# The first head of attention opened with transposes in place of shift transfers, and the end of attention in another order

## The chip, the cores and the metric

One core of a Trainium2 chip runs the whole program. The metric is the device time of one execution in microseconds; the kernel before took a median of 728.87 us in three runs (727.69 to 729.34).

## The reference

Three stages follow each other: attention that only looks at keys of the same hash bucket, a gated layer, and a layer of experts of which each token uses one. The change touches the first and the point where it meets the second.

```python
# q, k, v: [2, 8, 768, 64]; proj: [64, 6]
q_bits = (einsum('bhsd,dk->bhsk', q, proj) > 0)       # and k_bits alike
q_bucket = sum(q_bits * 2 ** arange(6), axis=-1)      # and k_bucket alike
mask = q_bucket[:, :, :, None] == k_bucket[:, :, None, :]
scores = where(mask, scale * q @ k.T, -1e9)
attn = softmax(scores)
x = (attn @ v) as [1536, 512]
x = ((x @ w_a) * (x @ w_b)) @ w_out                   # w_a, w_b: [512, 1536], w_out: [1536, 512]
out = experts(x)                                      # 8 experts, one per token, with a gate
```

## The kernel before

**Units.** Attention works on 8 pairs of heads (`pairs`; pair i has two heads j), each head in 3 units of 256 queries: 48 units, `NU`. In unit u two tiles of 128 queries (t = 0, 1) go through `scores` (L205: Q x K, with the sum over 64 numbers, for the two halves of the keys on the two row halves of TensorE; L208: a product of the sign bits, which lifts keys of the same bucket by a large number), `rowmax` on VectorE (L213), `expo` on ACT (L219), `normal` on GpSimd (L231), `turn` on VectorE (L238, a transpose in blocks of 32) and, in two groups of 12 blocks for each head, `pv` on TensorE (L250). The score banks are two tiles of `ps_s`; scores of unit u + 1 wait for the exponentials of unit u.

**Operands.** `load` fetches a pair's K and Q rows into `raw`; `turned` turns them with TensorE (L114) into K and Q, with the first head's 64 numbers on partitions 0 to 63 and the second's on 64 to 127. A score tile needs one half of the keys on the other 64 partitions: `swap` makes the shifted copies QS and KS with DMAs on SP (L104, L106). `signs` multiplies by the random directions (L181, L161 or L163) and takes signs on ACT (L154): sk for keys, from which KF is made by two factors (L145), and QF and QG for queries. For pair 0 all of this stands ahead of the loop over the units: K and Q are turned and evicted whole, four swaps are issued, the queries' signs are taken in four passes. For later pairs it is spread over the units.

**What sets the order.** Each engine runs its instructions in the order in which the program issues them; there is no scheduler. The loop over u in `attention` issues rows and exponentials, scores, preparations, transposes and pv, and calls `hook(u, place)` at five places. `tile_kernel` hangs other work there:

- `plan` and `places` hold the steps that split the first weights of the gated layer from 64-bit words into two 32-bit parts (`split64`): fetch (L431, SP), rest (L436) and top (L439) on VectorE, low (L445, ACT), add (L450, GpSimd), size (L455, ACT), guard (L461, VectorE), parts (L466 ACT, L467 GpSimd). The last two jobs (`outs`) are the halves of w_out; their scratch tile `late` lies in the buffer of `raw`, so it is free once the last pair is turned (unit 34), and the second half's fetch waits for the first half's parts.
- `fill` says after which units gated products are issued on TensorE (L536): a number 2 is one group of 12 matmuls over 384 columns. Up to unit 46 they use a bank of pv; from NU on a score bank. Their evictions are held back until the next `hook(u, 2)`.

The last units are: pv of head 14, first group, at u = 47 and second group at u = 48; two groups of pv of head 15 behind the loop, between `hook(NU + 2, 0)`, `hook(NU + 3, 0)` and `hook(NU + 4, 0)`. `epilogue` (L270) empties the pv banks of a head with four copies on ACT before the next head's pv may write them.

Of the kernel before, what the change touches and what calls it, by code (L numbers as in the profile page):

```python
# [8 lines left out]
F32 = mybir.dt.float32  # L9
F32R = mybir.dt.float32r  # L10
BF16 = mybir.dt.bfloat16
I32 = mybir.dt.int32
U32 = mybir.dt.uint32
AF = mybir.ActivationFunctionType
ALU = mybir.AluOpType
# [10 lines left out]
class Kernel:  # L26
# [37 lines left out]
    def attention(self, xh, xl, pools, hook):  # L64
        nc = self.nc
        sb, ps_s, ps_pv = pools
        NB = self.proj.shape[1]
        S, D = self.S, self.D
        NC = S // 128
# [3 lines left out]
        H2 = S // 2  # L73
# [6 lines left out]
        raw, Q, QS, K, KS, QF, QG, KF, VR = {}, {}, {}, {}, {}, {}, {}, {}, {}  # L80

        def load(i, qs=(nc.sync, nc.sync)):
            b, hp = pairs[i]
            t = raw[i] = sb.tile([128, 2, NC, 2, D], F32, tag="raw", name="raw", bufs=1)
            for j in range(2):
                for n, src in ((1, self.k), (0, self.q)):
                    qs[n].dma_start(out=t[:, n, :, j, :], in_=src[b, 2 * hp + j].rearrange("(p c) d -> p c d", c=NC))

        def load_v(h):
            (b, hp), j = pairs[h // 2], h % 2  # L90
# [10 lines left out]
        def swap(i, n, a):  # L101
            x, y = slice(64 * a, 64 * a + 64), slice(64 - 64 * a, 128 - 64 * a)
            if n == 0:
                nc.sync.dma_start(out=QS[i][x], in_=Q[i][y])  # L104
            else:
                nc.sync.dma_start(out=KS[i][x], in_=K[i][y, a * H2:(a + 1) * H2])  # L106
# [4 lines left out]
        def turned(i, n):  # L111
            p = pvb[n]
            for c in range(NC):
                nc.tensor.transpose(  # L114
                    p[:, c // 3, c % 3 * 128:c % 3 * 128 + 128], raw[i][:, n, c].rearrange("p h d -> p (h d)"), self.ident
                )
            if n == 0:
                Q[i] = sb.tile([128, S], F32, tag="q", name="q", bufs=2)
                QS[i] = sb.tile([128, S], F32, tag="qs", name="qs", bufs=2)
            else:  # L120
                K[i] = sb.tile([128, S], F32, tag="k", name="k", bufs=2)
                KS[i] = sb.tile([128, H2], F32, tag="ks", name="ks", bufs=2)
            dst = halves((Q, K)[n][i])

            def out(eng, swaps=True):
                scale = float(D) ** -0.5 if n == 0 else 1.0
                if eng is nc.scalar:
                    nc.scalar.mul(dst, p[:, :, :H2], scale)
                else:
                    eng.tensor_scalar(dst, p[:, :, :H2], scale, None, ALU.mult)  # L130
                if swaps:
                    for a in (1, 0):
                        swap(i, n, a)

            return out

        later = []

        def masks(eng=nc.scalar):
            for kf, sk in later:  # L140
                for j in range(2):
                    if eng is nc.scalar:
                        eng.mul(kf[:, j], sk, self.fac[:, j:j + 1])
                    else:
                        eng.tensor_scalar(kf[:, j], sk, self.fac[:, j:j + 1], None, ALU.mult)  # L145
            later.clear()

        def signs(i, n):
            p = pvb[n]
            lz = self.lz.rearrange("p a b c -> p (a b c)")  # L150
            half = [slice(64 * x, 64 * x + 64) for x in range(2)]

            def sign(dst, src):
                nc.scalar.activation(dst, src, AF.Sign, bias=self.bias[:src.shape[0]], scale=2.0 ** 100)  # L154

            if n == 0:
                QF[i] = sb.tile([128, H2], BF16, tag="qf", name="qf", bufs=2)
                QG[i] = sb.tile([128, H2], BF16, tag="qg", name="qg", bufs=2)
                for x, r in enumerate(half):
                    if i == 0:  # L160
                        nc.tensor.matmul(p[:, x, :H2], lz, Q[i][:, x * H2:(x + 1) * H2], start=True, stop=True)  # L161
                    else:
                        nc.tensor.matmul(  # L163
                            p[r, 0, :H2], lz[:, r], Q[i][:, x * H2:(x + 1) * H2], start=True, stop=True, tile_position=(0, 64 * x)
                        )

                def out(*_):
                    if i == 0:
                        for x in range(2):
                            sign(QF[i][half[x]], p[half[x], x, :H2])  # L170
                            sign(QG[i][half[1 - x]], p[half[1 - x], x, :H2])
                        return
                    sign(QF[i], p[:, 0, :H2])
                    for x in range(2):
                        nc.sync.dma_start(out=QG[i][half[1 - x]], in_=QF[i][half[x]])

                return out
            KF[i] = sb.tile([128, 2, H2], BF16, tag="kf", name="kf", bufs=2)
            sk = sb.tile([128, H2], BF16, tag="sk", name="sk", bufs=1)
            for x, r in enumerate(half):  # L180
                nc.tensor.matmul(  # L181
                    p[r, 0, :H2], lz[:, r], K[i][:, x * H2:(x + 1) * H2], start=True, stop=True, tile_position=(0, 64 * x)
                )

            def out(*_):
                sign(sk, p[:, 0, :H2])
                later.append((KF[i], sk))

            return out
# [94 lines left out]
        NU = len(units)  # L284
# [6 lines left out]
        for j in range(2):  # L291
            d = slice(64 * j, 64 * j + 64)
            for x in range(2):
                nc.vector.tensor_copy(self.lz[d, x, j, :NB], self.pr[d])
        turns = turned(0, 1), turned(0, 0)
        turns[0](nc.scalar, False)
        turns[1](nc.vector, False)
        for a in (1, 0):
            for n in (1, 0):
                swap(0, n, a)  # L300
        load(1)
        hook(-1, 0)
        load_v(0)
        preps = signs(0, 1), signs(0, 0)
        for prep in preps:
            prep()
        masks(nc.vector)
        scores(0, 0)
        scores(0, 1)
        preps = []  # L310
        finish = (
            (1, finish_add, (cols[0],)), (2, finish_add, (cols[1],)), (2, finish_high, (cols[0],)),
            (3, finish_low, (cols[0],)), (3, finish_high, (cols[1],)), (4, finish_low, (cols[1],)),
# [717 lines left out]
def tile_kernel(ctx, tc, q, k, v, proj, w_a, w_b, w_out, emb, tau, w1, w2, out, dbg=None):  # L1031
# [5 lines left out]
    with tc.manual_schedule():  # L1037
# [15 lines left out]
        with tc.tile_pool(name="conv", bufs=1, side="left") as X.conv, \  # L1053
                tc.tile_pool(name="att", bufs=2, side="right") as sb, \
                tc.tile_pool(name="ps_s", bufs=2, space=PSUM) as ps_s, \
                tc.tile_pool(name="ps_pv", bufs=1, space=PSUM) as ps_pv:

            def spare():
                return X.mid.tile([128, 4 * 384], F32R, tag="g", name="spare")

            def late():
                return sb.tile([128, 2 * S], F32, tag="raw", name="late", bufs=1)

            jobs = [X.load_first(w, f, spare) for f in range(2) for w in range(2)]
            outs = [X.load_first(2, f, late) for f in range(2)]


            plan = {(-1, 0): [jobs[0][0], jobs[1][0]], (36, 1): [outs[0][0]], (45, 1): [outs[1][0]]}
            places = (
                (3, 4, 5, 6, 6, 7, 9), (8, 8, 9, 10, 12, 13, 15), (16, 17, 18, 21, 21, 22, 27), (20, 23, 24, 28, 30, 31, 33),  # L1070
                (38, 38, 39, 40, 41, 41, 45), (NU, NU, NU, NU + 1, NU + 1, NU + 1, NU + 2),
            )
            for (_, steps), us in zip(jobs + outs, places):
                for m, u in enumerate(us):
                    plan.setdefault((u, 3 if m in (3, 4, 6) else 4), []).append(steps[m])
            plan[13, 0], plan[16, 0] = [jobs[2][0]], [jobs[3][0]]
            first = [(t, f, w, h) for t in range(2) for f in range(2) for w in range(2) for h in range(2)]


            fill = {40: 2, 43: 2, 46: 2, NU: 2, NU + 2: 2, NU + 3: 2, NU + 4: 4}  # L1080

            held = []

            def hook(u, at):
                if at == 2:
                    while held:
                        held.pop(0)()
                for job in plan.pop((u, at), []):
                    job()
                if at == 0:  # L1090
                    for n in range(fill.get(u, 0)):
                        t, f, w, half = first.pop(0)
                        if half == 0:
                            X.part = K.banks[(2, 0)[n // 2]] if u < NU else K.bank()
                        X.gated_products(0, t, f, w, half, X.part, held if u < NU + 2 else None)

            K.attention(X.xh, X.xl, (sb, ps_s, ps_pv), hook)
            assert not plan and not first
# [189 lines left out]
```

## Time and profile before

| | us |
|---|---|
| median of 3 runs | 728.87 |
| lowest, highest | 727.69, 729.34 |
| the profiled execution, time | 727.76 |
| its span | 726.0 |
| TensorE busy in it | 697.9 (96%) |
| VectorE busy | 459.0 (63%) |
| ACT busy | 354.1 (49%) |
| GpSimd busy | 415.5 (57%) |
| attention, about | the first 230 of the span |

A row of a timeline has the start from the span's beginning, the duration, the engine (PE is TensorE, DVE VectorE, POOL GpSimd, SPq the issue of a DMA by SyncE), the line, what it writes and reads, and, in brackets, how long the engine was idle before and what released it. Releasers are inferred from semaphores. [...] "Issue" is time in which the engine waited for nothing that the profile shows.

### The profile page before, as it was taken

Reading aid. Unit: us, or ns where it says so; the run is one execution under the profiler, and the core shown is the slowest. Engines: PE = TensorE matmul, PEld = TensorE weight load, DVE = VectorE, ACT = ScalarE, POOL = GpSimd, SP = SyncE. Lnnn points to the kernel's source line nnn. Section 1 sums busy time; section 2 is a strip of 40 time slices with the busy share of each in tenths; the row PEclk is TensorE's granted clock in tenths of the full one; section 3 lists DMA queues with packets and bytes.
Section 4 is the critical chain, followed back from the end, with each engine's and each line's share of the span. In section 5 each row is a group of like instructions: output and inputs, shape, how many; then the busy total and the mean of one; then the engine's idle time right before and its main releaser. Section 6 shows DMA issues by size and latency. Waiting matters only on the chain.

```text
span 726.0 us, 16193 instructions
## 1 busy us (share of the span) xinstructions
PE 697.9 (96%) x6793; PEld 586.9 (81%) x6793; DVE 459.0 (63%) x669; ACT 354.1 (49%) x658; POOL 415.5 (57%) x343
## 2 busy tenths in 40 slices
PE   7799999997989999999999999999999999999996
PEld 5455656564768989999999999998889899889995
DVE  3999999997984535646545556434744855555650
ACT  3778888886753342222121212143446556556551
POOL 0668778875773563745646626545424766656651
PEclk9999999999999999999999999999999999999999
DMA  6948744633341230311111301443332866577510
GB/s 143 220 111 177 162 119 117 164 84 98 71 133 60 72 105 5 113 59 58 59 60 59 112 4 59 157 162 116 113 134 79 290 215 219 196 240 241 202 54 23
DMA packets 68603, 88.29 MB, mean 122 GB/s; under 512 B 28963, under 2 KB 41123, under 8 KB 68528
## 3 DMA queue, kind: packets, MB, share of 16 engines
q1 hardware_dynamic: 63888, 78.71, 37.5%
q0 software_dynamic: 2560, 7.34, 2.7%
q10 hardware_dynamic: 2080, 1.18, 0.5%
q8 instruction: 54, 0.88, 0.5%
q14 instruction: 21, 0.17, 0.1%
HBM read 75.52 MB, written 7.34 MB: 114 GB/s over the span
## 4 chain that ended last, share of the span: by engine, by line
PE 77%; DVE 10%; ACT 5%; issue 3%; DMA 3%; POOL 1%; SPq 1%; POOLq 0%; DVEq 0%
PE ab L536 24%; PE yp L568 13%; PE op L912 11%; PE hp L862 10%; PE pv L250 6%; PE st L205 4%; DVE nm L213 4%; DVE et L238 3%; ACT e L219 3%; PE part L536 2%; PE hr L880 2%; PE xgt L839 1%; PE pv L536 1%; PE st L208 1%; DMA raw<-in_k_dram 1%
## 5 line engine op out<-in xcount | busy, mean ns | idle before, releaser
L536 PE MATMUL ab<-xh,w 128*128 128x384 f32 x704 | 185.7, 338 | 0.0
L536 PEld LDWEIGHTS ab<-xh,w 128*128 128x128 f32 x704 | 127.7, 188 | 2.1 <-issue 1.2
L231 POOL TENSOR_SCALAR e<-e,s,mc 128x768 f32<-128x768 f32 x96 | 93.8, 988 | 46.3 <-ACT e L219 38.2
L536 PE MATMUL ab<-xl,w 128*128 128x384 f32 x352 | 118.3, 336 | 0.0
L551 POOL TENSOR_TENSOR g<-a,g 128x384 fp32r<-128x384 f32 x48 | 56.4, 1176 | 107.2 <-ACT g L550 107.2
L818 POOL TENSOR_TENSOR w<-raw,w 128x1024 fp32r<-128x1024 f32 x36 | 88.0, 2447 | 39.2 <-ACT w L817 37.7
L568 PE MATMUL yp<-w,g 128*128 128x512 f32 x432 | 103.3, 391 | 1.0 <-DVE a L549 0.7
L219 ACT ACTIVATE e<-st,nm 128x768 f32<-128x768 f32 x96 | 85.8, 898 | 36.4 <-DVE r L223 25.7
L213 DVE TENSOR_REDUCE nm<-st 128x1 f32<-128x768 f32 x96 | 89.5, 937 | 11.2 <-PE st L208 10.8
L568 PEld LDWEIGHTS yp<-w,g 128*128 128x128 f32 x432 | 80.3, 188 | 16.6 <-DVE a L549 1.0
L205 PE MATMUL st<-ks,qs 64*128 64x384 f32 x192 | 83.7, 516 | 9.4 <-ACT e L219 9.1
L205 PE MATMUL st<-k,q 64*128 64x384 f32 x192 | 84.2, 519 | 4.6 <-ACT e L219 4.5
L238 DVE STREAM_TRANSPOSE et<-e 128x1536 f32<-128x1536 f32 x48 | 84.9, 1768 | 0.0
L912 PE MATMUL op<-w,hth 128*128 128x512 f32 x256 | 80.7, 397 | 0.0
L862 PE MATMUL hp<-xgh,w 128*128 128x256 f32 x448 | 80.7, 281 | 0.0
L250 PEld LDWEIGHTS pv<-et,vr 32*64 32x64 f32 x3072 | 60.7, 132 | 20.5 <-issue 11.1
L550 ACT CAST g<-a 128x384 fp32r<-128x384 f32 x48 | 24.7, 515 | 107.8 <-DVE a L549 107.8
L250 PE MATMUL pv<-et,vr 32*64 32x192 f32 x3072 | 72.7, 329 | 4.3 <-issue 2.3
L818 DVE TENSOR_TENSOR w<-raw,w 128x1024 fp32r<-128x1024 f32 x28 | 64.9, 2319 | 14.6 <-ACT w L817 14.3
L862 PEld LDWEIGHTS hp<-xgh,w 128*128 128x128 f32 x448 | 69.2, 188 | 0.3
L545 ACT COPY a<-ab 128x384 f32<-128x384 f32 x44 | 20.9, 476 | 95.6 <-PE ab L536 94.4
L536 PEld LDWEIGHTS ab<-xl,w 128*128 128x128 f32 x352 | 66.2, 188 | 0.8
(201 smaller groups left out, 1232.2 us busy)
## 6 DMA issues: line engine op xcount, KB each, us to landing
raw<-in_moe_w_dram SPq DMA_DIRECT2D x32, 1024.0 KB, 5.2
vr<-in_v_dram SPq DMA_DIRECT2D x64, 192.0 KB, 3.8
raw<-in_moe_w_a_dram SPq DMA_DIRECT2D x5, 1024.0 KB, 5.3
raw<-in_moe_w_b_dram SPq DMA_DIRECT2D x5, 1024.0 KB, 5.1
raw<-in_moe_w_out_dram SPq DMA_DIRECT2D x5, 1024.0 KB, 5.0
raw<-in_k_dram SPq DMA_DIRECT2D x16, 192.0 KB, 4.8
qs<-q SPq DMA_DIRECT2D x16, 192.0 KB, 3.7
raw<-in_q_dram SPq DMA_DIRECT2D x14, 192.0 KB, 4.1
```

Source lines behind the costliest of these rows:

```text
L205: nc.tensor.matmul(st[:, n, :H2], q[d, ql], k[d], start=True, stop=False, tile_position=(64 * n, 0))
L213: nc.vector.tensor_reduce(NM[u][:, t:t + 1], ST[u, t][:, :, :H2], axis=AX.XY, op=ALU.max, negate=True)
L219: nc.scalar.activation(halves(E[u][:, t]), ST.pop((u, t))[:, :, :H2], AF.Exp, bias=NM[u][:, t:t + 1], accum_out=SU[u][:, t:t + 1])
L231: nc.gpsimd.tensor_scalar(E[u][:, t], E[u][:, t], r[:, t:t + 1], c[:, t:t + 1], ALU.mult, ALU.add)
L238: nc.vector.transpose(ET[h][:, :, 2 * g:2 * g + 2].rearrange("p b c s -> p c b s"), E.pop(u).rearrange("p c (b s) -> p c b s", s=32),)
L250: nc.tensor.matmul(pvb[a // 2][m:m + 64, a % 2, :NC * 32], v[d], et[d, n].rearrange("p c s -> p (c s)"), start=(n < 2), stop=(n >= NB32 - ...
L536: nc.tensor.matmul(p[:, :384], w[:, k, fs], x[:, k, cols], start=(k == 0 and n == 0), stop=(k == self.KD - 1 and n == 2),)
L551: nc.gpsimd.tensor_tensor(gl[:, f], a, f32(gh[:, f]), ALU.subtract)
L568: nc.tensor.matmul(p, g[:, f, rows], w[:, f], start=(n == 0), stop=(n == 5))
L818: eng.tensor_tensor(l, raw, f32(h), ALU.subtract)
L862: nc.tensor.matmul(p[:, :256], w[:, k, fs], x[:, k], start=(n == 0), stop=(n == 3 * self.KD - 1))
L912: nc.tensor.matmul(p, h[:, 2 * n + f, rows], w[:, f], start=(n == 0 and f == 0 and m == 0), stop=(n == 3 and f == 1 and m == 2),)
```

## The change

`opening` replaces the preparation of pair 0. `raw` now holds K ahead of Q, so that 128 columns that begin 64 earlier are one head's numbers of one block and the other head's of the block before: turned by TensorE, they put the first head on partitions 64 to 127. Three such transposes fill a bank (`first`): two sets for Q, one for the second half of K. VectorE evicts Q in two halves and QS's upper half in two pieces, ACT evicts K and KS's upper half. Only the swaps into the lower halves remain as DMAs. Signs of queries 0 to 383 are taken at once; those of 384 to 767 (`rest`) are multiplied behind the scores of unit 0 and taken on ACT after its second exponential.

At the end of attention the fetch of the first half of w_out goes from unit 36 to 35 and its first step from 38 to 37; the steps of the second half, but for the first, go one step later; the 12 matmuls of `fill` at NU + 2 go to unit 47, into a score bank.

```diff
--- before.py
+++ after.py
@@ -84,7 +84,7 @@
             t = raw[i] = sb.tile([128, 2, NC, 2, D], F32, tag="raw", name="raw", bufs=1)
             for j in range(2):
                 for n, src in ((1, self.k), (0, self.q)):
-                    qs[n].dma_start(out=t[:, n, :, j, :], in_=src[b, 2 * hp + j].rearrange("(p c) d -> p c d", c=NC))
+                    qs[n].dma_start(out=t[:, 1 - n, :, j, :], in_=src[b, 2 * hp + j].rearrange("(p c) d -> p c d", c=NC))

         def load_v(h):
             (b, hp), j = pairs[h // 2], h % 2
@@ -112,7 +112,7 @@
             p = pvb[n]
             for c in range(NC):
                 nc.tensor.transpose(
-                    p[:, c // 3, c % 3 * 128:c % 3 * 128 + 128], raw[i][:, n, c].rearrange("p h d -> p (h d)"), self.ident
+                    p[:, c // 3, c % 3 * 128:c % 3 * 128 + 128], raw[i][:, 1 - n, c].rearrange("p h d -> p (h d)"), self.ident
                 )
             if n == 0:
                 Q[i] = sb.tile([128, S], F32, tag="q", name="q", bufs=2)
@@ -134,6 +134,79 @@

             return out

+        def opening():
+            scale = float(D) ** -0.5
+            half = [slice(0, 64), slice(64, 128)]
+            keys, queries = slice(0, H2), slice(H2, S)
+            lz = self.lz.rearrange("p a b c -> p (a b c)")
+            for t, tag, n in ((Q, "q", S), (QS, "qs", S), (K, "k", S), (KS, "ks", H2)):
+                t[0] = sb.tile([128, n], F32, tag=tag, name=tag, bufs=2)
+            for t, tag in ((QF, "qf"), (QG, "qg")):
+                t[0] = sb.tile([128, H2], BF16, tag=tag, name=tag, bufs=2)
+            KF[0] = sb.tile([128, 2, H2], BF16, tag="kf", name="kf", bufs=2)
+            sk = sb.tile([128, H2], BF16, tag="sk", name="sk", bufs=1)
+            twice = [ps_s.tile([128, 2, 512], F32, tag="s", name="twice") for _ in range(2)]
+
+            flat = raw[0].rearrange("p n c h d -> p (n c h d)")
+
+            def rows(p, n, c):
+                nc.tensor.transpose(
+                    p[:, c // 3, c % 3 * 128:c % 3 * 128 + 128], flat[:, S * (1 - n) + 128 * c:][:, :128], self.ident
+                )
+
+            def first(p, n, c):
+                nc.tensor.transpose(
+                    p[:, c // 3, c % 3 * 128:c % 3 * 128 + 128], flat[:, S * (1 - n) + 128 * c - 64:][:, :128], self.ident
+                )
+
+            def out(dst, src, k=scale):
+                nc.vector.tensor_scalar(dst, src, k, None, ALU.mult)
+
+            def sign(dst, src):
+                nc.scalar.activation(dst, src, AF.Sign, bias=self.bias[:src.shape[0]], scale=2.0 ** 100)
+
+            for c in range(NC):
+                rows(pvb[1], 1, c)
+            nc.scalar.copy(halves(K[0]), pvb[1][:, :, :H2])
+            for c in range(3):
+                rows(pvb[0], 0, c)
+            out(Q[0][:, keys], pvb[0][:, 0, :H2])
+            for c in range(3):
+                first(twice[0], 0, c)
+            out(QS[0][half[1], keys], twice[0][half[1], 0, :H2])
+            for c in range(3, NC):
+                first(twice[1], 1, c)
+            nc.scalar.copy(KS[0][half[1]], twice[1][half[1], 1, :H2])
+            for c in range(3, NC):
+                rows(pvb[0], 0, c)
+            out(Q[0][:, queries], pvb[0][:, 1, :H2])
+            for c in range(3, NC):
+                first(pvb[1], 0, c)
+            for x, r in enumerate(half):
+                nc.tensor.matmul(
+                    pvb[1][r, 0, :H2], lz[:, r], K[0][:, x * H2:(x + 1) * H2], start=True, stop=True, tile_position=(0, 64 * x)
+                )
+            sign(sk, pvb[1][:, 0, :H2])
+            nc.tensor.matmul(pvb[0][:, 0, :H2], lz, Q[0][:, keys], start=True, stop=True)
+            for x in range(2):
+                sign((QF, QG)[x][0][half[x]], pvb[0][half[x], 0, :H2])
+            for j in range(2):
+                nc.vector.tensor_scalar(KF[0][:, j], sk, self.fac[:, j:j + 1], None, ALU.mult)
+            out(QS[0][half[1], queries], pvb[1][half[1], 1, :H2])
+            for n in (1, 0):
+                swap(0, n, 0)
+
+            def rest():
+                nc.tensor.matmul(pvb[0][:, 1, :H2], lz, Q[0][:, queries], start=True, stop=True)
+
+                def out(*_):
+                    for x in range(2):
+                        sign((QF, QG)[1 - x][0][half[x]], pvb[0][half[x], 1, :H2])
+
+                return out
+
+            return rest
+
         later = []

         def masks(eng=nc.scalar):
@@ -157,19 +230,11 @@
                 QF[i] = sb.tile([128, H2], BF16, tag="qf", name="qf", bufs=2)
                 QG[i] = sb.tile([128, H2], BF16, tag="qg", name="qg", bufs=2)
                 for x, r in enumerate(half):
-                    if i == 0:
-                        nc.tensor.matmul(p[:, x, :H2], lz, Q[i][:, x * H2:(x + 1) * H2], start=True, stop=True)
-                    else:
-                        nc.tensor.matmul(
-                            p[r, 0, :H2], lz[:, r], Q[i][:, x * H2:(x + 1) * H2], start=True, stop=True, tile_position=(0, 64 * x)
-                        )
+                    nc.tensor.matmul(
+                        p[r, 0, :H2], lz[:, r], Q[i][:, x * H2:(x + 1) * H2], start=True, stop=True, tile_position=(0, 64 * x)
+                    )

                 def out(*_):
-                    if i == 0:
-                        for x in range(2):
-                            sign(QF[i][half[x]], p[half[x], x, :H2])
-                            sign(QG[i][half[1 - x]], p[half[1 - x], x, :H2])
-                        return
                     sign(QF[i], p[:, 0, :H2])
                     for x in range(2):
                         nc.sync.dma_start(out=QG[i][half[1 - x]], in_=QF[i][half[x]])
@@ -292,22 +357,13 @@
             d = slice(64 * j, 64 * j + 64)
             for x in range(2):
                 nc.vector.tensor_copy(self.lz[d, x, j, :NB], self.pr[d])
-        turns = turned(0, 1), turned(0, 0)
-        turns[0](nc.scalar, False)
-        turns[1](nc.vector, False)
-        for a in (1, 0):
-            for n in (1, 0):
-                swap(0, n, a)
+        rest = opening()
         load(1)
         hook(-1, 0)
         load_v(0)
-        preps = signs(0, 1), signs(0, 0)
-        for prep in preps:
-            prep()
-        masks(nc.vector)
         scores(0, 0)
         scores(0, 1)
-        preps = []
+        preps, held_kind = [rest()], None
         finish = (
             (1, finish_add, (cols[0],)), (2, finish_add, (cols[1],)), (2, finish_high, (cols[0],)),
             (3, finish_low, (cols[0],)), (3, finish_high, (cols[1],)), (4, finish_low, (cols[1],)),
@@ -1065,10 +1121,10 @@
             outs = [X.load_first(2, f, late) for f in range(2)]


-            plan = {(-1, 0): [jobs[0][0], jobs[1][0]], (36, 1): [outs[0][0]], (45, 1): [outs[1][0]]}
+            plan = {(-1, 0): [jobs[0][0], jobs[1][0]], (35, 1): [outs[0][0]], (45, 1): [outs[1][0]]}
             places = (
                 (3, 4, 5, 6, 6, 7, 9), (8, 8, 9, 10, 12, 13, 15), (16, 17, 18, 21, 21, 22, 27), (20, 23, 24, 28, 30, 31, 33),
-                (38, 38, 39, 40, 41, 41, 45), (NU, NU, NU, NU + 1, NU + 1, NU + 1, NU + 2),
+                (37, 38, 39, 40, 41, 41, 45), (NU, NU + 1, NU + 1, NU + 2, NU + 2, NU + 2, NU + 3),
             )
             for (_, steps), us in zip(jobs + outs, places):
                 for m, u in enumerate(us):
@@ -1077,7 +1133,7 @@
             first = [(t, f, w, h) for t in range(2) for f in range(2) for w in range(2) for h in range(2)]


-            fill = {40: 2, 43: 2, 46: 2, NU: 2, NU + 2: 2, NU + 3: 2, NU + 4: 4}
+            fill = {40: 2, 43: 2, 46: 2, 47: 2, NU: 2, NU + 3: 2, NU + 4: 4}

             held = []

@@ -1091,7 +1147,7 @@
                     for n in range(fill.get(u, 0)):
                         t, f, w, half = first.pop(0)
                         if half == 0:
-                            X.part = K.banks[(2, 0)[n // 2]] if u < NU else K.bank()
+                            X.part = K.banks[(2, 0)[n // 2]] if u < NU - 1 else K.bank()
                         X.gated_products(0, t, f, w, half, X.part, held if u < NU + 2 else None)

             K.attention(X.xh, X.xl, (sb, ps_s, ps_pv), hook)
```

## Rows read from the trace of the kernel before

**Rows 1.** page: busy time by engine, and DMA queue q8

```profile
...
PE 697.9 (96%) x6793; PEld 586.9 (81%) x6793; DVE 459.0 (63%) x669; ACT 354.1 (49%) x658; POOL 415.5 (57%) x343
...
q8 instruction: 54, 0.88, 0.5%
...
```

**Rows 2.** stretches: us, then busy us of PE, PEld, DVE, ACT, POOL; PEclk

```profile
...
40.00:100.00 60.00, 56.95 (x1190) 35.29 (x1188) 58.79 (x82) 50.79 (x106) 45.61 (x57) 1.00 0.60 140
173.50:176.00 2.50, 2.48 (x12) 0.86 (x12) 2.47 (x3) 1.41 (x3) 2.17 (x3) 0.74 0.03 7
176.00:179.30 3.30, 3.30 (x100) 2.65 (x100) 2.71 (x3) 1.98 (x4) 1.89 (x2) 0.68 0.00 0
216.00:219.00 3.00, 3.00 (x11) 3.00 (x11) 0.40 (x1) 1.50 (x3) 0.00 (x0) 0.50 0.00 0
...
```

**Rows 3.** timeline of the opening: start, us, engine, instruction [idle]

```profile
...
6.79 1.80 PE L114 MATMUL pv<-ident,raw 128*128 128x128 f32 x12 [0.50 <-DMA raw<-in_k_dram]
...
8.88 0.87 PE L181 MATMUL pv<-k,lz 128*64 128x384 f32 x4 [0.29 <-issue]
...
9.68 1.56 PE L161 MATMUL pv<-q,lz 128*128 128x384 f32 x4
...
11.28 0.58 ACT L154 ACTIVATE qf<-pv,bias 64x384 bf16<-64x384 f32 x1 [0.90 <-PE pv L161]
...
12.45 0.56 PE L205 MATMUL st<-ks,qs 64*128 64x384 f32 x1 [0.37 <-DMA qs<-q]
...
12.46 0.33 PE L208 MATMUL st<-kf,qf 64*128 64x384 bf16 x1
...
13.53 1.82 DVE L213 TENSOR_REDUCE nm<-st 128x1 f32<-128x768 f32 x2 [2.57 <-PE st L208]
...
17.67 0.90 ACT L219 ACTIVATE e<-st,nm 128x768 f32<-128x768 f32 x1 [1.28 <-DVE nm L213]
...
```

**Rows 4.** timeline of SP, VectorE and TensorE around unit 38

```profile
...
156.63 1.19 SPq L104 DMA_DIRECT2D qs<-q  x2
...
164.20 0.43 SPq L431 DMA_DIRECT2D late<-in_moe_w_out_dram  x1
...
163.36 0.96 DVE L213 TENSOR_REDUCE nm<-st 128x1 f32<-128x768 f32 x1 [0.31 <-PE st L208]
...
170.36 0.43 DVE L436 TENSOR_SCALAR late<-late 128x512 int32<-128x512 int32 x1 [3.35 <-DMA qg<-qf]
...
173.52 0.59 PE L205 MATMUL st<-ks,qs 64*128 64x384 f32 x1 [3.58 <-ACT e L219]
...
```

**Rows 5.** chain that ended last, past the last unit: start, us, what

```profile
...
207.96 3.80 PE pv L250 x168
211.77 2.33 issue
...
214.96 5.94 PE part L536 x24
220.90 2.14 PE pv L250 x96
223.04 2.28 PE part L536 x12
...
```

**Rows 6.** DMA queues, 205 to 211.7 and 211 to 213: packets, MB, share

```profile
...
q1 hardware_dynamic: 1041, 2.03, 102.2%
...
q8 instruction: 1, 0.02, 3.1%
...
```

**Rows 7.** timeline of VectorE and ACT at the end of attention

```profile
...
213.36 1.76 DVE L238 STREAM_TRANSPOSE et<-e 128x1536 f32<-128x1536 f32 x1
...
215.01 0.48 ACT L270 COPY xp<-pv 64x384 f32<-64x384 f32 x1 [3.33 <-PE pv L250]
...
```

**Rows 8.** DMA queues in 86.5 to 87.5

```profile
...
q1 hardware_dynamic: 858, 0.22, 129.7%
q8 instruction: 1, 0.02, 8.2%
...
```

## The prediction

> **What bounds the kernel now.** I read the page's totals first, then a table of stretches, then the timeline of three places where TensorE stands still. TensorE is busy 96% of the span, and while attention runs it and VectorE are both nearly full: 56.95 and 58.79 us of the 60 between 40 and 100 us [rows 1, 2]. So a hole in either is lost for good, and work taken off another engine brings nothing. The change touches three such holes, and all lie before the gated stage. What follows starts when attention ends (the buffers of its weight loads come free there), so a gain in attention moves everything behind it.
>
> The first is **the opening**. The last operand to arrive before the first scores is QS, shifted by a DMA: the second half of the first score starts at 12.45, with that transfer as its releaser, and the first row maximum at 13.53 [rows 3].
>
> The second lies in **units 38 and 39**. VectorE stood 3.35 us before L436 (170.36), the first step of splitting the first half of w_out. The row names a qg transfer as releaser, but L436 doesn't read qg; it reads the tile `late`, whose fetch was issued only at 164.20, behind the four V loads. Behind L436 on VectorE stood the row maxima of unit 39, so the exponentials, so the score banks: TensorE waited 3.58 us for ACT's e, until 173.52 [rows 4]. [...]
>
> The third lies **past the last unit's scores**. Two pv groups follow each other on TensorE, and at 211.77 it stops for 2.33 us inside the second, on no wait that the profile shows ("issue") [rows 5]. After it the clock is 0.50 from 216 to 219 [rows 2], and the 24 gated matmuls there take 5.94 us where 12 take 2.28 at full clock [rows 5]. What I take the stop to be: queue q8 moves 54 packets of 16 KB, one per 13,586 / 54 = 252 of TensorE's matmuls and weight loads together [rows 1], so it carries TensorE's instructions. Between 205 and 211.7 the data queue q1 holds the DMA engines at 102% (two weight loads of 1.5 MB, behind V) and q8 has no packet; the next one starts between 211 and 213 [rows 6]. The engine ran dry. [...]
>
> **Opening, part by part.** Removed from the path: the DMA, and two of the four sign passes of the queries. Added: nine transposes on TensorE. Twelve took 1.80 us, so nine take 9 x 0.15 = 1.35, and they end at 6.79 + 1.80 + 1.35 = 9.95. Behind them come the key signs (0.87, now 10.8), then the sign product for the first half of the queries alone, half of 1.56 (11.6). ACT's QF and QG, 0.58 us each, end at 12.8, and the mask product of 0.33 behind the second ends at 13.1 [rows 3]. The first row maximum starts at 13.1 instead of 13.53: **0.4 us gained**. The evictions in pieces run beside these transposes and products; ACT's 64-row copy takes 0.48 [rows 7], and without that cover each would cost about that. If the transposes overlap better the gain is 1.0; no row shows transposes across the two halves of raw, and at twice the price 0.9 is lost. I take the rate of the nearest row. The two moved sign passes, 1.1 us on ACT, now run after unit 0's second exponential, where ACT has stood idle 1.28 us [rows 3]; the second scores of unit 1 wait for them on TensorE, with the last sign product and the next pair's transposes queued behind. Without that cover they cost up to 1.1, and 0.1 is what I leave for them. On SP two shift transfers go away and the two others, needed only in unit 3, stay ahead of the next pair's loads, which start earlier. Net **0.3 us**.
>
> **Fetch of the first half of w_out one unit earlier, its first step from unit 38 to 37.** On SP the issue (0.43) now follows the swaps of unit 35, which end at 157.8, and stands before the V loads, which wait for a pv product of unit 36 anyway: no cost. From issue to use it took 6.2 us beside 0.75 MB of V; from 157.9 that gives 164.1 at worst. VectorE comes to it when it leaves unit 37's transpose, at 163.36 - 0.31 = 163.05 [rows 4]; so it waits 1.1 us at worst. With no V beside it I expect it there in time. The step's 0.43 moves into a unit where VectorE idles 0.31 before its row maximum [rows 4]. With the stop gone TensorE doesn't wait its 3.58 before 173.52. The slow clock behind it cost 2.5 x 0.26 + 3.3 x 0.32 = 1.7 [rows 2]. Together 5.3; the second step, L439, stays in VectorE's way in unit 38, so I take **5.1 us**. Ends: 1.5 if the data lands late and the clock falls all the same, 5.3 if all goes.
>
> **End of attention.** Twelve gated matmuls move from behind the last unit's second pv group to between the two groups. TensorE's work is the same. From 207.96 to 220.90 it took 12.94 us for two pv groups (2 x 2.14) and 24 matmuls (2 x 2.28), 8.84 together: 4.1 are lost [rows 5]. Will it still run dry? The late packet depends on the loads, so I let it come at the same distance behind them, and TensorE goes on at 214.10 as before. It has 18 instructions more behind it (nine transposes with their weight loads) and 24 of the moved matmuls, so it runs dry 42 of 192 instructions earlier in a pv group (0.47 us), but 2.28 us of matmuls stand before it: 211.77 + 2.28 - 0.47 = 213.6. A rest of 0.5 us remains. Between 40 and 100 us TensorE idled 3.05 us in short pieces with a clock of 1.00 [rows 2], so I let 0.5 cost no clock. **3.6 us gained**; ends 0 (a stop as long as before, clock too) and 4.1. The first pv of the last head now comes at about 217 instead of 220.90. It needs VectorE's last transpose (213.36 + 1.76) and ACT's four copies that empty the banks (4 x 0.48 behind the pv group that ends at 214.7: 216.6) [rows 7]; both are there, by 0.4 us. The transpose has help: the step `top` of the last w_out half now goes behind it. The last step of that split (ACT, POOL) goes behind one more gated group; a pv group and 24 matmuls (2.14 + 4.56) still lie before the first yp, which reads it, so it costs nothing. The second `late` fetch and w_a keep their places on SP.
>
> **Sum.** 0.3 + 5.1 + 3.6 = 9.0. The profiled execution took 727.76 (span 726.0), so 718.8; the median of the three runs shown is 1.1 above it, which gives 719.9. I say **719.3**, between them.
>
> **Rivals.**
> A. The end keeps its stop: the moved matmuls only put it elsewhere. For it: the packet is late whatever TensorE does. Against: 2.28 us of matmuls with few instructions is what a dry engine needs. The 3.6 is gone: 722.9.
> B. VectorE still waits in unit 37, because L436 waits for something else than its own fetch (the profile names qg). Against: the tile it reads is not qg's. Of 5.1 some 4.5 are gone: 723.8.
> C. Slower. The 18 instructions more shift every later block. The q8 packet near 87 us comes while q1 has the DMA engines at 130% [rows 8], and two more near 111 and 135 us look alike; an engine with little left in its buffer runs dry there as at 211.77. Each costs up to 4.1 us with its clock. It decides the sign from three full stops: 3 x 4.1 - 9.0 = +3.3, 732.2. Against: the shift is 18 of 252 instructions, and TensorE idles only 3.05 us between 40 and 100 us in all [rows 2].
> D. The opening brings nothing, because its chain of TensorE and ACT is as long as the DMA was: 719.6, inside the range.
>
> **How the numbers follow.** Forecast with D 0.72, A 0.13, B 0.08, C 0.04, and 0.03 for a change whose parts cancel and end near 729. The range takes in the best ends (0.9 + 5.3 + 4.1 = 10.3, so 717.4 by the profiled execution, less 0.7 for the spread of the runs) and both A and B: 716.7 to 723.9. Something like 0.2%, 1.5 us, is what a measurement of this kernel can tell from no change. Faster 0.93, same 0.03, slower 0.04.
>
> **What would show it.** Right: the first row maximum at about 13.1; no idle before VectorE's first L436 on `late`, and a granted clock of 1.00 from 160 to 180; twelve matmuls between the two last pv groups; a TensorE gap of under 1 us in the second group. Wrong: an L436 that still waits over 1 us; a gap of 2 us anywhere in the pv groups with a clock of 0.5 behind it; ACT's copies holding the last head's pv. If attention ends 9 us earlier and the span doesn't, something behind attention was late already.

## The result, and the profile after

The changed kernel took a median of 718.65 us in six runs (718.08 to 719.59), the kernel before 727.97 beside it; the ratio is 0.9882, 95% interval 0.9856 to 0.9908. Forecast were 719.3 and 716.7 to 723.9. The span of the profiled execution fell from 726.0 to 717.3.

The third stop first, since its term fits best. The chain of the changed kernel from the last unit on (start, us, what):

```profile
200.83 2.31 PE pv L592 x12
...
203.70 2.20 PE pv L315 x92
205.90 2.28 PE part L592 x12
208.18 2.58 PE pv L315 x96
210.76 2.29 PE part L592 x12
213.05 2.14 PE pv L315 x96
```

L592 is L536 of before, L315 is L250. Against [rows 5] the stop of 2.33 us is gone; the second pv group takes 2.58 where an undisturbed one takes 2.14, so 0.44 us are left (0.5 forecast), and no slow clock follows: the clock granted to TensorE (PEclk, the third number from a row's end, as a share of full speed) is 1.00 from 200 to 215, where it was 0.50 from 216 to 219 before [rows 2].

```profile
200.00:215.00 15.00, 14.90 (x332) 12.22 (x328) 10.51 (x13) 8.22 (x18) 9.73 (x12) 1.00 0.53 159
```

The last head's pv starts at 213.05, and what it needed was there:

```profile
209.09 1.77 DVE L303 STREAM_TRANSPOSE et<-e 128x1536 f32<-128x1536 f32 x1
...
212.28 0.48 ACT L335 COPY co<-pv 64x384 f32<-64x384 f32 x1
```

VectorE's last transpose ended at 210.86, ACT's last copy at 212.76: 0.3 us to spare, where 0.4 was reckoned from [rows 7].

Units 37 to 39, by SP's and VectorE's timeline and TensorE's:

```profile
158.48 0.53 SPq L487 DMA_DIRECT2D late<-in_moe_w_out_dram  x1
...
163.71 0.63 DVE L492 TENSOR_SCALAR late<-late 128x512 int32<-128x512 int32 x1
...
167.81 1.06 DVE L495 SCALAR_TENSOR_TENSOR late<-late 128x512 int32<-128x512 int32 x1
168.80 0.94 DVE L278 TENSOR_REDUCE nm<-st 128x1 f32<-128x768 f32 x1
...
170.88 0.59 PE L270 MATMUL st<-ks,qs 64*128 64x384 f32 x1 [0.38 <-ACT e L284]
```

The fetch stands at 158.48, L492 (L436 of before, 3.35 us idle ahead of it in [rows 4]) starts with no idle time in its row, and TensorE's wait of 3.58, for the exponentials of unit 39, is one of 0.38. That VectorE keeps the order of the program shows in the kernel before: the scores of unit 39 had ended at 167.81, and their row maxima, which stand behind L436, began at 171.43.

```profile
167.48 0.32 PE L208 MATMUL st<-kf,qf 64*128 64x384 bf16 x1
...
171.43 0.95 DVE L213 TENSOR_REDUCE nm<-st 128x1 f32<-128x768 f32 x1
```

The granted clock of the changed kernel, in the two stretches of [rows 2] that had 0.74 and 0.68 and in the one ahead of them:

```profile
170.00:173.50 3.50, 3.12 (x75) 1.68 (x68) 3.50 (x6) 2.42 (x6) 2.20 (x4) 1.00 0.07 17
173.50:176.00 2.50, 2.50 (x83) 1.87 (x71) 2.44 (x3) 2.46 (x6) 1.55 (x2) 1.00 0.00 0
176.00:179.30 3.30, 3.30 (x20) 2.44 (x20) 3.27 (x5) 3.24 (x8) 2.98 (x5) 1.00 0.98 232
```

The opening, by TensorE's timeline, VectorE's first row maximum and ACT's row of unit 1:

```profile
6.44 1.17 PE L153 MATMUL pv<-ident,raw 128*128 128x128 f32 x9 [0.59 <-DMA raw<-in_k_dram]
...
9.07 0.87 PE L186 MATMUL pv<-k,lz 128*64 128x384 f32 x4
9.87 0.91 PE L190 MATMUL pv<-q,lz 128*128 128x384 f32 x2
...
12.05 0.33 PE L273 MATMUL st<-kf,qg 64*128 64x384 bf16 x1 [0.27 <-ACT qg L166]
...
12.42 1.82 DVE L278 TENSOR_REDUCE nm<-st 128x1 f32<-128x768 f32 x2 [0.68 <-PE st L273]
...
16.57 0.90 ACT L284 ACTIVATE e<-st,nm 128x768 f32<-128x768 f32 x1 [0.22 <-DVE nm L278]
```

The last operand is now QG, as forecast, but the first row maximum comes 1.11 us earlier than at 13.53 [rows 3], not 0.4: 0.35 because this execution's rows landed sooner (6.44 for 6.79), 0.76 from the first transpose on. Not all of that is the opening's: in the six executions with the old opening in the table below this stretch takes 6.43 to 6.74, and the kernel before has the longest. Against their middle, 6.5, the opening gains 0.5. The 21 transposes overlap better than twelve let one think: the key signs start 2.63 us behind the first transpose, where 3.15 was reckoned. The moved sign passes just fit into ACT's idle time: 0.22 of 1.28 is left.

And it didn't last. Two waits took it back in this execution, one in the scores of unit 6 and one in a pv group (together 1.36 us):

```profile
35.26 0.33 PE L273 MATMUL st<-kf,qg 64*128 64x384 bf16 x1 [0.75 <-DMA qg<-qf]
...
89.94 1.38 PE L315 MATMUL pv<-et,vr 32*64 32x192 f32 x53 [0.61 <-issue]
```

The table takes each execution apart at marks of its timeline, in us: from the start of the first transposes of raw to the row maxima of units 0, 6 and 37, from there to unit 47, to the first yp (the gated layer's product with w_out), and to the first op (the experts' output product). It has all kernels of the next section. The medians are of four batches of runs, in the order of the rows: the first two rows, the next four, the next four, the last three. The kernel before had 727.97, 727.17, 727.89 and 726.88 in them.

| kernel | unit 0 | unit 6 | unit 37 | 37 to 47 | to yp | to op | median |
|---|---|---|---|---|---|---|---|
| before | 6.74 | 28.96 | 152.62 | 44.91 | 28.22 | 303.73 | 727.97 |
| changed | 5.98 | 29.19 | 153.53 | 40.09 | 24.63 | 303.10 | 718.65 |
| opening_only | 5.99 | 28.48 | 151.79 | 45.08 | 28.33 | 303.12 | 726.71 |
| end_only | 6.44 | 28.84 | 152.48 | 40.10 | 24.65 | 303.11 | 717.88 |
| early_fetch_only | 6.43 | 28.64 | 151.93 | 40.10 | 28.24 | 303.76 | 722.09 |
| fill_only | 6.64 | 28.85 | 153.05 | 45.52 | 24.43 | 303.12 | 723.38 |
| after_again | 5.98 | 28.48 | 151.86 | 40.11 | 25.13 | 303.72 | 718.55 |
| count_restored | 6.10 | 29.70 | 152.88 | 40.08 | 24.42 | 303.13 | 718.81 |
| v_later | 5.98 | 28.48 | 152.43 | 40.11 | 24.80 | 303.70 | 718.88 |
| wa_late | 6.56 | 29.17 | 152.44 | 45.52 | 24.50 | 304.96 | 725.50 |
| after_third | 5.98 | 28.98 | 152.54 | 40.10 | 24.77 | 303.12 | 718.90 |
| end_only_again | 6.44 | 28.65 | 152.50 | 40.09 | 24.37 | 303.13 | 718.09 |
| both_mended | 5.98 | 28.47 | 152.35 | 40.10 | 24.62 | 303.12 | 718.79 |

### The profile page after: what moved, and what is told of

It is laid out like the page before. It is cut to its first block, busy times and chain, and to the rows that moved or that the text cites. A ratio compares the mean times of both kernels' runs of the same rounds, so it can differ in the third digit from the quotient of the medians.

```text
span 717.3 us, 16210 instructions
## 1 busy us (share of the span) xinstructions
PE 695.9 (97%) x6802; PEld 584.6 (82%) x6802; DVE 463.8 (65%) x672; ACT 354.8 (49%) x659; POOL 415.2 (58%) x343
## 4 chain that ended last, share of the span: by engine, by line
PE 79%; DVE 11%; ACT 4%; issue 3%; DMA 3%; POOL 0%; SPq 0%; POOLq 0%; DVEq 0%
PE ab L592 25%; PE yp L624 14%; PE op L968 11%; PE hp L918 10%; PE pv L315 6%; DVE nm L278 5%; PE st L270 4%; DVE et L303 4%; ACT e L284 2%; PE hr L936 2%; PE part L592 2%; PE st L273 1%; PE xgt L895 1%; PE pv L592 1%; DMA late<-in_moe_w_out_dram 1%
## 5 line engine op out<-in xcount | busy, mean ns | idle before, releaser
L592 PE MATMUL ab<-xh,w 128*128 128x384 f32 x704 | 185.7, 338 | 0.0
L592 PEld LDWEIGHTS ab<-xh,w 128*128 128x128 f32 x704 | 127.7, 188 | 2.0 <-issue 1.2
L592 PE MATMUL ab<-xl,w 128*128 128x384 f32 x352 | 118.3, 336 | 0.0
L607 POOL TENSOR_TENSOR g<-a,g 128x384 fp32r<-128x384 f32 x48 | 53.5, 1115 | 102.4 <-ACT g L606 102.4
L874 DVE TENSOR_TENSOR w<-raw,w 128x1024 fp32r<-128x1024 f32 x28 | 67.4, 2406 | 13.5 <-ACT w L873 13.5
L315 PEld LDWEIGHTS pv<-et,vr 32*64 32x64 f32 x3072 | 60.2, 130 | 18.2 <-issue 9.4
L315 PE MATMUL pv<-et,vr 32*64 32x192 f32 x3072 | 72.5, 326 | 2.3 <-ACT q L128 1.6
L629 DVE TENSOR_TENSOR y<-yp,y 128x512 f32<-128x512 f32 x60 | 41.5, 692 | 39.2 <-PE yp L624 39.2
```

The costliest lines, as they stand in the source:

```text
L315: nc.tensor.matmul(pvb[a // 2][m:m + 64, a % 2, :NC * 32], v[d], et[d, n].rearrange("p c s -> p (c s)"), start=(n < 2), stop=(n >= NB32 - ...
L592: nc.tensor.matmul(p[:, :384], w[:, k, fs], x[:, k, cols], start=(k == 0 and n == 0), stop=(k == self.KD - 1 and n == 2),)
L607: nc.gpsimd.tensor_tensor(gl[:, f], a, f32(gh[:, f]), ALU.subtract)
L874: eng.tensor_tensor(l, raw, f32(h), ALU.subtract)
```

## The experiments

**The parts one by one.** opening_only has the diff without its last three hunks; end_only has these alone; the two others divide them:

```diff
 # early_fetch_only
-plan = {..., (36, 1): [outs[0][0]], ...}      places: (38, 38, 39, ...)
+plan = {..., (35, 1): [outs[0][0]], ...}      places: (37, 38, 39, ...)
 # fill_only
-fill = {40: 2, 43: 2, 46: 2, NU: 2, NU + 2: 2, ...}          (NU, NU, NU, NU + 1, NU + 1, NU + 1, NU + 2)
+fill = {40: 2, 43: 2, 46: 2, 47: 2, NU: 2, ...}              (NU, NU + 1, NU + 1, NU + 2, NU + 2, NU + 2, NU + 3)
-X.part = ... if u < NU else K.bank()
+X.part = ... if u < NU - 1 else K.bank()
```

> Of the change only the fetch of the first half of w_out at unit 35 and its first step at unit 37. Theory: VectorE does not wait before that step, the clock stays at 1.00 from 160 to 180, unit 42 comes 5.2 us earlier; the stop of 2.3 us between the last pv groups and its slow clock stay. About 5 us under before, 722 to 723. Rival (VectorE waited for the qg transfer): the wait comes back in unit 37 or 38 and the gain is under 2 us.

> Of the change only the twelve matmuls at unit 47 and the later steps of the second half of w_out. Theory: VectorE still waits 3.4 us in unit 38; the stop in the last pv groups falls from 2.3 us to 0.8 at most, without a slow clock; the first yp comes 3.6 us earlier, about 724 to 725. Rival (the stop is no matter of fetched instructions and moves along): the gap of over 2 us is there in the second group, gain under 1 us.

> The opening as before, with the new end of attention. Theory: no gap near 89 us; unit 37's row maximum at 159.4 as before, unit 42 some 5.2 us earlier than before (179.7), the first yp some 8.8 us earlier (223.7); 0.6 us under the changed kernel, about 717.5 to 718.5. Rival (the opening carries its 1.1): about 1 us over the changed kernel, 719.5 to 720.

> The new opening with the end of attention as before. Theory: the head start of 1.1 us at the first row maximum is lost by unit 20 as in the changed kernel (0.2 left at unit 6, half a us behind at unit 20, with a TensorE gap of 0.6 us inside a pv group near 89 us), so the row maximum of unit 37 comes within 0.6 us of 160.0; unit 39 still waits for the late fetch and the stop in the last pv groups is still there. Profiled time 0 to 1 us over before, about 728. Rival (the opening is a gain of its own that the end only covers): unit 37 at 158.3 and 1.1 us under before.

Early fetch: 722.09 us, ratio 0.992 (0.9895 to 0.9944). VectorE's row in its timeline, and the stop that stays, in its chain:

```profile
162.34 0.76 DVE L436 TENSOR_SCALAR late<-late 128x512 int32<-128x512 int32 x1
```

```profile
206.26 2.35 issue
208.61 0.87 PE pv L250 x20
209.48 5.93 PE part L536 x24
```

No wait before L436, and units 37 to 47 take 4.8 us less. By itself this doesn't tell the fetch from the qg transfers, since L436 now stands ahead of them too. The trace of the kernel before does (their issue by SP, and the time from issue to landing):

```profile
167.65 1.11 SPq L175 DMA_DIRECT2D qg<-qf  x2
```

```profile
DMA to landing us min/median/max: 2.9/3.1/3.3
```

Neither transfer had landed before 167.65 + 2.9 = 170.5, and L436 started at 170.36, so it wasn't qg that it waited for. Fill: 723.38, ratio 0.9938 (0.9914 to 0.9963). Its VectorE still waits in unit 38, and its chain has no stop:

```profile
171.43 0.43 DVE L436 TENSOR_SCALAR late<-late 128x512 int32<-128x512 int32 x1 [4.10 <-DMA qg<-qf]
```

```profile
208.90 2.20 PE pv L250 x92
211.09 2.29 PE part L536 x12
213.38 2.36 PE pv L250 x96
215.75 2.30 PE part L536 x12
```

Each of the two removes its own stop and leaves the other; with the second, unit 47 to yp is 3.8 us shorter. (It also moves steps of the second half of w_out; no run has the twelve matmuls alone.) Both together, end_only: 717.88 (717.35 to 718.43), ratio 0.9854 (0.9803 to 0.9905), with 4.8 and 3.6 us in the same two columns. The parts add. For the opening alone the theory failed: there was no gap near 89 us, and unit 37 came 0.83 us sooner behind the first transposes than in the kernel before, as the rival had it. But early_fetch_only, with the old opening, is as early there (151.93), and the time went neither way: it is 726.71, ratio 0.9993 (0.997 to 1.0016), which can't be told from no change.

**Is the stop a late packet?** The load of w_a goes to ACT's queue, behind attention:

```diff
+if c == 1 and w == 0:
+    X.queue = nc.scalar      # fetch() issues on X.queue
+    fetch()
+    X.queue = nc.sync
+else:
     after(at, fetch)
```

> The kernel before with the 1 MB load of w_a issued by ACT behind attention's last copies in place of SP at 205.7 us. Theory (the 2.3 us stop between the last pv groups is a late instruction packet, held up by the loads): with 1 MB less in the data queue the packet comes some 2 to 3 us sooner after its request and the stop falls under 1 us, with no slow clock behind it. Rival (the stop is no fetch, or the packet is slow by itself): 2.3 us as before. The total says little, since w_a may now be late for its conversion.

The chain at the last pv groups:

```profile
208.34 3.81 PE pv L250 x168
212.15 0.17 issue
212.32 0.87 PE pv L250 x20
213.18 4.38 PE part L537 x24
```

The stop stands at the same instruction (168 before it, 20 behind) but lasts 0.17 us, and the 24 matmuls take 4.38 in place of 5.94, at a granted clock of 1.00:

```profile
213.18:217.56 4.38, 4.38 (x33) 4.13 (x34) 3.31 (x4) 3.39 (x7) 2.55 (x3) 1.00 0.01 4
```

The place of the stop is a count of instructions. In opening_only, with nine more matmuls (and their weight loads) in the opening, it comes eight matmuls sooner, and in after_again, the changed kernel once more, a short rest of it stands behind 92 + 12 + 56, the same count, though twelve of these are other matmuls:

```profile
207.12 3.51 PE pv L315 x160
210.63 2.70 issue
213.33 0.90 PE pv L315 x28
```

```profile
202.39 2.20 PE pv L315 x92
204.59 2.28 PE part L592 x12
206.87 1.46 PE pv L315 x56
208.33 0.42 issue
208.75 1.20 PE pv L315 x40
```

Its end follows the packet. The table has the matmuls ahead of the stop as the chain counts them, its times, and where the packet of q8 starts (in us, and from the row maxima of unit 47):

| kernel | matmuls ahead | stop begins | packet starts | from unit 47 | TensorE goes on | behind the packet's start |
|---|---|---|---|---|---|---|
| before | 168 | 211.77 | 211.78 | 7.45 | 214.10 | 2.32 |
| early_fetch_only | 168 | 206.26 | 206.26 | 7.44 | 208.61 | 2.35 |
| opening_only | 160 | 210.63 | 210.90 | 7.42 | 213.33 | 2.43 |
| end_only | 168 | 208.76 | 206.44 | 7.29 | 208.95 | 2.51 |
| after_again | 160 | 208.33 | 206.39 | 7.64 | 208.75 | 2.36 |
| wa_late | 168 | 212.15 | 209.93 | 5.23 | 212.32 | 2.39 |

In all six TensorE goes on 2.3 to 2.5 us after the packet starts, and only where w_a was moved does the packet start sooner, by 2.2 us. So these rows have the stop as instructions that came late, and 1 MB of data in front of them as what made them late (2.33 us with it, 0.17 without); the rival is out. Unit 47 to yp is 3.7 us shorter, though no work was moved. The median, 725.5, is only 2.4 us under the 727.89 beside it, since w_a is late for its conversion (VectorE waits 5.25 us for it at 234.4, and the stretch from yp to op is 1.2 us longer).

**Where the opening's head start goes.**

```diff
 # count_restored: 13 instructions in place of 22, so that later ones lie where they lay
-for m in range(22): nc.tensor.transpose(pvb[0][...], self.ident, self.ident)
+for m in range(11): nc.tensor.matmul(pvb[0][:, m % 2], one[:, :128], <one, 512 columns>, start=True, stop=True)
+for m in range(2): nc.tensor.transpose(pvb[0][:, m % 2, :128], self.ident, self.ident)
 # v_later
-if s == 0 and u >= 3 and ...: load_v(u // 3)
+if s == 0 and u >= 6 and ...: load_v(u // 3)
+if u == 4: load_v(1)
```

after_again and after_third are the changed kernel, end_only_again is end_only, both_mended has both edits above. The 22 transposes, which stand ahead of those of raw, took 421 ns each (median) in the kernel before, the 96 of raw behind them 273, at a granted clock of 1.00; that they warm TensorE up is the expectations' reading; no run leaves them out.

> The changed kernel once more, beside the next ones on one chip. Theory (the 18 more instructions of the opening make the packet near 87 us come too late for a pv group): the TensorE gap near 89 us is there again, 0.3 to 0.9 us, and unit 37's row maximum comes at about 160. Rival (that gap hangs on how the transfers of one execution fall, as the opening alone, which has the same instructions, showed none): no gap, unit 37 near 158.7, and the span 1 us shorter.

> The changed kernel with the 22 transposes that warm TensorE up replaced by 11 matmuls of 512 columns and 2 transposes of about the same length, so that every later instruction lies where it lay before. Theory: the packet near 87 us is in time, no gap of over 0.3 us inside a pv group near 89 us, unit 21 keeps what unit 18 had; 0.8 us under the changed kernel. Rival (the gap is the transfers' doing): a gap or none as in the changed kernel, time the same within 0.4 us.

> The changed kernel with the four loads of the second head's V issued in unit 4, behind the transfers of pair 1's query signs, in place of unit 3 ahead of them. Theory (the opening's head start of 0.8 us at unit 3 ends in unit 6 because those signs land when the data queue is through with V, whatever the opening does): TensorE no longer waits 0.75 us for them near 35 us, unit 6 keeps 0.7 to 0.9 us over before in place of 0.1; up to 0.7 us under the changed kernel. Rival (the signs are late for another reason): the wait stays.

> The changed kernel, timed in five rounds beside the two below. Theory (the opening's first row maximum comes 0.5 to 0.75 us sooner behind the first transposes, and the transfers of the next 80 us take or give up to 0.9 us from one execution to the next): 718 to 719, within 0.5 us of the kernel without the opening. Rival (the new opening costs time in the end, as the medians so far say, 718.6 against 717.9): 0.5 us or more over it.

> The new end with the opening as before, beside the changed kernel. Theory: the first row maximum 6.4 to 6.7 us behind the first transposes in place of 6.0; 718 to 718.6, within 0.5 us of the changed kernel. Rival (the opening costs): 717.9 again, the changed kernel 0.5 us or more over it.

> The changed kernel with the later V loads and the wide warming matmuls together. Theory (both losses of the opening's head start, at unit 6 and near 89 us, come from transfers, and each change takes one away): no wait of over 0.2 us at unit 6, no gap near 89 us, unit 37 within 152.0 us of the first transposes in place of 153.5; 717.3 to 718.3, the least of the three. Rival (the losses fall elsewhere when one place is mended): 718.5 to 719 like the rest.

after_again went the rival's way in attention: the same program, neither wait, unit 37 at 158.65 and 1.67 us less from the first transposes than in the first execution. Its span wasn't 1 us shorter, though: it was 717.2, since the rows landed 0.35 later and the stretches to yp and op took 0.5 and 0.6 more. In count_restored the gap near 89 us was gone, but unit 6 lost more:

```profile
35.85 0.33 PE L273 MATMUL st<-kf,qg 64*128 64x384 bf16 x1 [1.15 <-ACT q L128]
```

In v_later the wait at unit 6 was gone. But after_again had neither wait without either edit, so neither run shows that its edit did it, and neither is faster than after_again (718.81 and 718.88, 718.55 beside them): both theories missed. Nor is the wait at unit 6 the new opening's: after_third has one of 0.54 us, and wa_late, with the old opening, one of 0.42:

```profile
35.54 0.33 PE L208 MATMUL st<-kf,qg 64*128 64x384 bf16 x1 [0.42 <-DMA qg<-qf]
```

both_mended had neither of the two waits, but a new one in a pv group, and took 718.79, a miss on the rival's side (the losses fall elsewhere):

```profile
42.42 0.58 PE L315 MATMUL pv<-et,vr 32*64 32x192 f32 x15 [0.55 <-issue]
```

v_later, the other kernel with the moved V loads, has 0.30 us there. Side by side the changed kernel (after_third) took 718.90 (718.16 to 720.73) and end_only_again 718.09 (717.88 to 719.09): 0.8 us, past the 0.5 of the rival, by which the opening costs time. Three medians of the first (718.65, 718.55, 718.90) lie above both of the second (717.88, 718.09), by 0.5 to 1.0 us, while the ranges overlap. The opening gains 0.46 us at the first row maximum over end_only and nothing that can be seen at the end; whether it costs half a microsecond, and by what, stays open.

## Why the prediction was right

The time lies 0.65 us under the forecast, and the two large terms were right by their own steps.

- **Fetch one unit earlier**: 5.1 forecast; units 37 to 47 took 44.91 before and 40.09 after, 4.8. early_fetch_only gives 4.8 in the same column and 5.1 in the median. The 0.3 that is missing lies within the scatter of that stretch: the other executions with the late fetch took 45.08 to 45.52. Of the 5.1, 1.7 were for the slow clock, from the 0.74 and 0.68 of [rows 2]; both stretches have 1.00 now. L439, which was to stay in VectorE's way, took 1.06 us in its new place, ahead of unit 39's row maxima (no run measures it apart). The landing was in time, and rival B falls with the row that shows no wait and with the qg transfers' landing in the kernel before.
- **End of attention**: 3.6 forecast, 28.22 - 24.63 = 3.6 measured. The assumption that the packet keeps its distance to the loads held (7.23 us from unit 47 to its start, 7.45 before), and the place of the stop was reckoned right too: 42 instructions, 21 matmuls, sooner in the group, and after_again has it 20 sooner (56 in place of 168 - 92 = 76). The engine still ran a little short, by 0.44 us here and 0.94 in after_again's second group. Rival A falls with fill_only, whose chain has no stop. In the kernel before no other "issue" stop of TensorE between the first row maximum and the end of attention is over 0.15 us; this one, with the DMA engines held at 102% by the data queue [rows 6], took 2.33 us with w_a in front, and 0.17 without.
- **Opening**: net 0.3 forecast. This term failed. At the first row maximum it gave 0.76 in this execution and 0.5 against the middle of the old opening's six, near the 0.4 reckoned. To unit 37 it had become a loss of 0.9 in the profiled execution. The step that failed was to let a head start in the opening count in full ("a gain in attention moves everything behind it"): for 80 us after it waits that hang on transfers, on QG of pair 1 (0.75 us) and, as far as the "issue" row tells, on the instruction packet near 87 us (0.61), set the time in some executions. From one execution to the next the stretch from the first transposes to unit 37 takes 151.9 to 153.1 us with the old opening and 151.8 to 153.5 with the new one, so 0.5 us can't be seen in it.
- **Rival C** (a block of instructions, a packet of q8, that comes late because of 18 more instructions) happened at its place, once, with 0.61 us and no slow clock (1.00 from 88 to 92); opening_only and after_again, with the same instructions, don't show it. The page's count is as reckoned, nine matmuls and nine weight loads more:

```profile
PE 695.9 (97%) x6802; PEld 584.6 (82%) x6802; DVE 463.8 (65%) x672; ACT 354.8 (49%) x659; POOL 415.2 (58%) x343
```

- **Behind attention** the forecast had nothing. 0.63 us more came there (303.73 to 303.10 from the first yp to the first op). early_fetch_only, v_later and after_again, which is the changed kernel itself, have the longer value too, so it isn't the change's.

The sum of the profiled executions: 0.35 (rows landed) - 0.91 (to unit 37) + 4.82 + 3.59 + 0.63 (yp to op) + 0.19 (experts) = 8.7, the difference of the spans. That it comes so near 9.0 is in part luck: the two terms that the runs bear out give 8.4, and what scatter took to unit 37 it gave back elsewhere.

The lowest medians of these runs are end_only's, the change without its new opening; whether that difference is real stays open, as said above.

## What to carry to other kernels

A stop of an engine on no visible wait, in a stretch dense in small instructions (here 2.33 us behind 168 matmuls in 3.80), can be its own instruction stream, as it was in this kernel: look whether an instruction packet starts shortly before the engine goes on (2.3 to 2.5 us here), whether the stop keeps its count of instructions when other work is put in front, and what the data queue was doing before. Either a few long instructions between the dense ones (0.44 us left in the changed kernel, no stop in fill_only) or a bulk load moved away (0.17 left in wa_late) took most of it here. And a microsecond won in an opening should be followed along the row maxima or the like before it is counted: work that hangs on transfers can take it back (0.75 us at unit 6 here, for QG).

## What was not expected

The slow clock came twice in attention of the kernel before, behind stops of 3.58 us (0.74 and 0.68 in the two stretches after it) and 2.33 us (0.50 from 216 to 219); in the changed kernel, with its longest gap inside attention 1.46 us, neither of the two is left: 1.00 from 13 to 215. And one program's executions differ by 1.7 us at unit 37 (153.53 and 151.86 from the first transposes), which the total hides: the two spans are 717.3 and 717.2. The place of a stop can be told in advance: nine more matmuls some 200 us earlier moved it by eight.
